# Fused attention and gated MLP on one core: down products, held P.V batches and the first tile of the last output chunk

## The chip, the core and the metric

The kernel runs on one core of a Trainium2 chip. The metric is the time of one execution in microseconds (us) on the device, as the median of several runs. Engines are called as in the profile: PE is TensorE's matmul, PEld its weight load, DVE is VectorE, ACT is ScalarE, POOL is GpSimd, SP is SyncE.

## The reference

The input `x` has 2048 rows of 640 values. It is normalised by row, and the normalised rows feed two branches whose product is added to `x`:

```python
xn = _layernorm(x, axis=-1)
# A: 32 heads of 20 columns
qkv = (xn @ wqkv).reshape(B, S, 3, H, Dh).transpose(2, 0, 3, 1, 4)
scores = einsum("bhqd,bhkd->bhqk", q, k) * Dh ** -0.5
o = einsum("bhqk,bhkd->bhqd", softmax(scores), v)
s = o.transpose(0, 2, 1, 3).reshape(B, S, D) @ wo
# B: F = 1728
h = sigmoid(xn @ w_gate) * (xn @ w_up)
g = silu(h @ w_down)
return x + s * g
```

All inputs and the output are bf16.

## The kernel before

The kernel is written as an instruction order for each engine, and the order comes from a planner in Python that runs when the program is built. The planner keeps a clock for PE (`pe[0]`), models ACT and DVE as queues of tasks with durations (`act`, `dve`), and decides at each step what PE does next.

**Passes.** The queries are cut into four chunks of 512 (`NQC`), the heads into eight groups of four (`NG`, `GH`): 32 passes. A pass holds 64 banks, one bank being the scores of 128 keys against 512 queries of one head, in one PSUM bank. PE computes scores by four row groups at once (L1280). The exponentials of a chunk of three or two banks are one ACT instruction (L1306), alternating between the PSUM sets `sc0` and `sc1`. A further bank can be put into one of two work banks (`misc0`, `misc1`, tile `spare`); DVE then computes its exponential by a cubic polynomial in four steps (L1326, L1347, L1351, L1357). `pv` (L1483) multiplies the probabilities by V, two banks for each head in a batch, and accumulates into `oacc`, the one PSUM bank for it. At the end of a pass DVE copies `oacc` out (`normalise`, L804), and the sums go through DRAM by POOL's DMAs to be inverted and spread.

**Jobs.** All else that PE has to do is a job, a generator that asks for a work bank, for something to be known, or for the time of its next matmul: Q, K and V products, `gateup_job` (gate and up products of one tile of 128 hidden columns into `hT`, with a tanh on ACT and a DVE product at L688), `down_job` (the products of `hT` with `w_down`, accumulated over the 14 tiles of the hidden dimension, L717, then tanh and a DVE product), `out_job` (the output projection of a finished chunk, L751) and the last chunk's jobs. The edge tile of 64 hidden columns is computed for two chunks at once, so an odd chunk's edge tile is made first, with the chunk before it. A job takes a work bank unless `spare_wanted` keeps it for DVE's scores. PE's time for a matmul of `n` columns in the down and output products is `mm_time(n)`.

**Zeros.** Where PE would have little to do, `zero_add` gives it a product with a zero matrix, added to `oacc` while its sum is open (L1459), or into a work bank that nobody uses (`unused`, L1465). `streamed()` is the planner's PE time within the last 3400 ns.

**The end.** The last pass is cut into parts of 256, 128 and 128 queries (`PARTS`). `part_job` computes the output projection of five of the eight head groups ahead for the four output tiles of the last chunk, gates it and has POOL add `x` by DMA (L791), so that `ahead[:, t4, :]` holds that part of the sum. `last_job` then turns the last pass's `oacc` copy (`oev`) with an identity product (L922), inverts the denominators (`rq`, L928), spreads them (`rb`, L933), turns them back (L950), scales (`oT`, L957), multiplies by the remaining rows of `wo` (L912), gates (`gated`, L997, two halves of 320 columns; for the last tile in one piece, L979), and `summed` adds `ahead` on DVE and has SP write the tile (L1001, L1002). The copy of the last part is on ACT (L897), planned by `take_part(len(PARTS) - 1, pe[0])` after the loop.

Of the kernel before, what the change touches and what calls it, by code (L numbers as in the profile page):

```python
# [12 lines left out]
ALU = mybir.AluOpType  # L13
# [3 lines left out]
PARTS = ((0, 256), (256, 128), (384, 128))  # L17
HEAD = 32
GH = 4
# [39 lines left out]
def kernel(  # L59
# [11 lines left out]
    nc = tc.nc  # L71
# [3 lines left out]
    S, D = x2.shape  # L75
# [3 lines left out]
    NFT = (F + P - 1) // P  # L79
# [4 lines left out]
    NQC = S // QC  # L84
    KT = S // P
# [6 lines left out]
    out_view = out2.rearrange("(p t) d -> p t d", t=TT)  # L92
# [84 lines left out]
    with tc.tile_pool(name="setup", bufs=1) as sp, \  # L177
# [167 lines left out]
        for word in ORDER.split():  # L345
            name, _, other = word.partition(":")
            kind, _, t = name.partition(".")
# [16 lines left out]

    MM5, MM3, MM1 = 216.0, 136.0, 70.0
    INTO = {"score": 100.0, "pv": 100.0, "fill": 100.0}
    WINDOW, ENOUGH, ZEROS, RESTED = 3400.0, 2500.0, 16, 400.0
    PE_OUT, SEM = 260.0, 70.0
    EXP_COL, EXP_FIX, EXP_LAG = 1 / 1.2, 52.0, 260.0
    DMA_WAIT, LANDED = 3400.0, 4000.0  # L370
# [48 lines left out]
    pe = [0.0]  # L419
# [27 lines left out]
    def streamed():  # L447
        while streams and streams[0][0] <= pe[0] - WINDOW:
            streams.pop(0)
        return sum(x[1] for x in streams)  # L450
# [7 lines left out]
    banks = [Cell(0.0), Cell(0.0)]  # L458
# [9 lines left out]
    def spare_wanted():  # L468

        free = sum(c.t is not None and c.t <= pe[0] for c in banks)  # L470
        return (free == 1 and not pressed() and next_round[0] - pe[0] < (KEEP_SPARE if at_bank[0] < SPARE_END else KEEP_LATE)
                and dve.backlog + dve.t - next_round[0] < D_BACKLOG)

    EARLY = 2
# [1 line left out]
    def pressed():  # L476
        return at_bank[0] <= EARLY * PER_PASS and any(x.due < at_bank[0] and x.left > 0.0 and (x.asks is None or x.asks[0] != "mm")
                                           for x in flight + jobs[:1])
# [163 lines left out]
    hTs, h_cells, d_cells, hEs = {}, {}, {}, {}  # L642
# [50 lines left out]
            h_cells.setdefault(c + k, []).append(tnh_free[-1])  # L693

    def mm_time(n):
        return max(n / 2.4 + 3.0, 100.0)

    def down_pieces(k):
        return [(t4, max(t4 * D, k * QC), min((t4 + 1) * D, (k + 1) * QC)) for t4 in range(QC // P)
# [2 lines left out]
    def down_job(c, k):  # L702
        last = c == NQC - 1
        yield "known", lambda: (bulk[0] == NFT and pe[0] > bulk_t[0] + LANDED and len(h_cells.get(c, [])) == NFT
                                and (not last or front() >= PER_PASS * (NG * c + k // 2 + 1)))
        yield "wait", h_cells[c]
        hT = hTs[c]
        if last:
            gq = gq_last[:, k * QC:(k + 1) * QC]
        else:  # L710
            gq = glu[0].tile([P, QC], FP32, tag="gqr", bufs=4, name="gq")
        held, psd = yield "bank",
        for t4, f0, f1 in down_pieces(k):
            for kf in range(NFT):
                rows = slice(0, P) if kf < NFT - 1 else slice(EDGE * (c % 2), EDGE * (c % 2 + 1))
                h_in = hT[:, kf, :] if kf < NFT - 1 else hEs[c]
                nc.tensor.matmul(psd[:, f0 - k * QC:f1 - k * QC], lhsT=h_in[rows, t4 * P:(t4 + 1) * P],  # L717
                                 rhs=glu[1][rows, kf, f0 - t4 * D:f1 - t4 * D], start=(kf == 0), stop=(kf == NFT - 1),
                                 skip_group_check=True)
                yield "mm", mm_time(f1 - f0), (f1 - f0) / 2.4  # L720
        d_cells.setdefault(c, []).append(Cell(pe[0]))
        made = {}

        def tanh():
            made["t"] = wk.tile([P, QC], BF16, tag="tnh", bufs=2, name="td")
            nc.scalar.activation(out=made["t"], in_=psd, func=ACT.Tanh, scale=0.25)  # L726

        def finish():
            nc.vector.scalar_tensor_tensor(out=gq, in0=made["t"], scalar=1.0, in1=psd, op0=ALU.add, op1=ALU.mult)
            if not last:  # L730
                nc.gpsimd.dma_start(out=gq_dram[c, :, k * QC:(k + 1) * QC], in_=gq)

        turned = act.add(480.0, [Cell(pe[0] + PE_OUT + 100.0), *tnh_free[-2:-1]], tanh, 0, EXP_LAG)
        tnh_free.append(dve.add(606.0, [turned], finish, 1))
        give_bank(held, tnh_free[-1])
        gq_cells[c, k] = tnh_free[-1]
# [29 lines left out]
    gq_last = kT_all[:, 0:3, :].rearrange("p g s -> p (g s)").bitcast(FP32)[:, 0:4 * D]  # L766
# [121 lines left out]
    def take_part(u, done):  # L888
        q0, width = PARTS[u]
        part = taken_parts[u] = {}  # L890

        def copy():
            part["oev"] = glu[0].tile([P, QC], FP32, tag="gqr", bufs=4, name="oev")[:, 0:width]
            if u < len(PARTS) - 1:
                nc.vector.tensor_copy(out=part["oev"], in_=oacc[:, q0:q0 + width])
            else:
                nc.scalar.activation(out=part["oev"], in_=oacc[:, q0:q0 + width], func=ACT.Identity)  # L897

        if u < len(PARTS) - 1:
            part["cell"] = dve.add(60.0 + width, [Cell(done + PE_OUT)], copy, -1)  # L900
        else:
            part["cell"] = act.add(52.0 + width * EXP_COL, [Cell(done + PE_OUT)], copy, -1, EXP_LAG)
        return part["cell"]

    def last_job(u):
# [13 lines left out]
        else:  # L919
            held, pd = yield "bank",  # L920
# [44 lines left out]
        for k, t4 in enumerate(tiles):  # L965
            got = []
            if final:
                if k:
                    outs = psum.tile([P, 3, 512], FP32, tag="sc0", bufs=1, name="outs")
                    for h in range(2):  # L970
                        out_mm(outs[:, h, 0:HALF], t4, h, NG - 2)
                        yield "mm", MM3
                for h in range(2):
                    out_mm(outs[:, h, 0:HALF], t4, h, NG - 1)
                    yield "mm", MM3

                def gate(t4=t4, outs=outs):
                    gq = gq_last[:, t4 * D:(t4 + 1) * D].rearrange("p (h d) -> p h d", h=2)
                    nc.vector.scalar_tensor_tensor(out=gq, in0=outs[:, 0:2, 0:HALF], scalar=0.25, in1=gq,  # L979
                                                   op0=ALU.mult, op1=ALU.mult)  # L980

                got.append(dve.add(740.0, [Cell(pe[0] + PE_OUT)], gate, -1))
            else:
                for h in range(2):
                    held, ps = yield "bank",
                    for g in range(PRE, NG):
                        out_mm(ps[:, 0:HALF], t4, h, g)
                        yield "mm", MM3
                    got.append(dve.add(400.0, [Cell(pe[0] + PE_OUT)], lambda t4=t4, h=h, ps=ps: gated(t4, h, ps), 1))
                    give_bank(held, got[-1])  # L990
                got.append(ending)
            dve.add(740.0, [out_cells[(NQC - 1) * 4 + t4], *got],
                    lambda t4=t4: summed(t4), -1 if final else 2)

    def gated(t4, h, ps):
        gq = gq_last[:, t4 * D:(t4 + 1) * D][:, h * HALF:(h + 1) * HALF]
        nc.vector.scalar_tensor_tensor(out=gq, in0=ps[:, 0:HALF], scalar=0.25, in1=gq, op0=ALU.mult, op1=ALU.mult)  # L997

    def summed(t4):
        ot = glu[0].tile([P, QC], FP32, tag="gqr", bufs=4, name="ot").bitcast(BF16)[:, 0:D]  # L1000
# [11 lines left out]
    K_COST, B_COST = 5 * MM5, 0.3 * MM5  # L1012
    GU_COST, DOWN_COST = 10 * MM5, NFT * (MM5 + 10.0)
    OUT_COST, PART_COST = NG * (MM5 + 10.0), 2 * (NG - 3) * MM3
    PART_DUE = [LAST-48 + 8 * t4 for t4 in range(4)]
    LAST_DUE = [e - 12 for e in ENDS[1:]] + [NB]
    WO_FROM, BULK_EVERY, bulk_t = 2, 6, [0.0]
    K_DUE, Q_DUE, B_DUE, V_DUE, OUT_DUE = -60, -50, -36, 6, 4 * PER_PASS
# [51 lines left out]
    glu = []  # L1070
# [114 lines left out]
    def held_job():  # L1185
        return any(x.asks is not None and x.asks[0] == "mm" and x.left < x.cost - 1 for x in flight)
# [245 lines left out]
    def pv_batch():  # L1432

        p = pv_pass[0]
        if p >= len(steps) - 1 + len(PARTS):
            return None
        if sum(pv_count[0]) == 0 and not (oacc_free[0].t is not None and oacc_free[0].t <= pe[0]):
            return None
        batch = []
        for j in range(GH):  # L1440
            mine = []
            for x in ready_p[j]:
                b, buf, i = x
                if unit(b) > p or len(mine) == 2:
                    break
                c, v = buf.made, v_cells.get((b % PER_PASS // GH, steps[min(p, len(steps) - 1)][1]))
                if c.t is not None and c.t + SEM <= pe[0] and v is not None and v.t is not None and v.t <= pe[0]:
                    mine.append(x)
            if len(mine) < 2:
                return None  # L1450
            batch.append(mine)
        return batch
# [61 lines left out]
    while pv_pass[0] < len(steps) - 1 + len(PARTS):  # L1514
# [37 lines left out]
        if b0 < NB and not stuck and alone(room):  # L1552
            idle = False
            credit = min(credit + per_bank(b0), 3000.0)
            continue
        batch = pv_batch()
        cost = PV_TIME + (INTO["pv"] if mode[0] != "pv" else 0.0)
        if batch and (cost <= room or held >= HELD):
            pv(batch)
# [23 lines left out]
        times = [until, pe[0] + 150.0] + [t + SEM for t in soon if t is not None]  # L1583
        pe[0] = min(t for t in times if t > pe[0] + 1.0)

    oacc_free[0] = take_part(len(PARTS) - 1, pe[0])
    while flight or jobs or timed or act.queue or dve.queue:
        advance(pe[0])
        if not fill(len(steps) - 1):
# [32 lines left out]
```

## Time and profile before

| | |
|---|---|
| median of 3 runs | 881.26 us (879.89 to 881.51) |
| the profiled execution, its own time | 878.75 us |
| its span in the profile | 877.1 us |
| granted clock of PE | 0.999 |
| ACT / DVE / PE busy | 861.9 / 837.9 / 799.4 us |
| exponentials on ACT | 355 of three banks, 356 of two |
| banks on DVE | 271 |

A busy time is the union of an engine's instructions. In a row of groups, the number after the bar is busy time and the mean of one instruction in ns, then the idle time just before these instructions and what ended it. In a row of the timeline, the first number is the start and the second the length of a stretch of equal instructions, in us.

### The profile page before, as it was taken

What the parts mean: (1) busy time and instruction counts of PE and PEld (TensorE: products, weight loads), DVE (VectorE), ACT (ScalarE), POOL (GpSimd) and SP (SyncE); (2) the same over time, 40 slices, a digit from 0 to 9 for tenths busy, and PEclk for the clock granted to TensorE, in tenths of its full rate; (3) what the DMA queues carried; (4) which work ended last, traced back from release to release, by engine and by line L of the source; (5) the groups of instructions that cost most, each with busy time, mean ns of one, the idle gap of its engine ahead of it and who ended that gap; (6) DMA issues with size and microseconds to landing.
All of it is one profiled execution on the core that took longest, in us unless ns stands there. A gap on an engine that the chain in (4) does not pass through costs nothing.

```text
span 877.1 us, 16778 instructions
## 1 busy us (share of the span) xinstructions
PE 799.4 (91%) x6358; PEld 286.2 (33%) x6440; DVE 837.9 (96%) x1164; ACT 861.9 (98%) x832; POOL 170.0 (19%) x314
## 2 busy tenths in 40 slices
PE   8999899999998999999999999989989989999997
PEld 3434333332222333222223332232223332233344
DVE  7799999999999999999999999999999999999996
ACT  7999999999999999999999999999999999999996
POOL 8401111101111113211101133111112231111110
PEclk9999999999999999999999999999999999999999
DMA  8212231125542124223321235313211443320111
GB/s 320 62 49 66 72 108 36 33 59 142 155 130 68 28 68 108 38 59 74 73 60 39 68 83 86 72 29 84 57 35 50 101 71 80 71 52 21 26 34 47
DMA packets 107303, 63.86 MB, mean 73 GB/s; under 512 B 78674, under 2 KB 101030, under 8 KB 107130
## 3 DMA queue, kind: packets, MB, share of 16 engines
q1 hardware_dynamic: 95270, 46.96, 20.1%
q0 software_dynamic: 11952, 15.83, 8.5%
q8 instruction: 50, 0.82, 0.4%
q14 instruction: 31, 0.25, 0.1%
HBM read 49.94 MB, written 16.11 MB: 75 GB/s over the span
## 4 chain that ended last, share of the span: by engine, by line
ACT 64%; issue 17%; PE 11%; DVE 6%; DMA 1%; POOL 0%; SPq 0%; ACTq 0%; DVEq 0%; POOLq 0%
ACT p L1306 60%; PE sc L1280 3%; ACT tnh L679 3%; PE work L667 2%; PE work L717 2%; PE oacc L1483 2%; DVE du L1351 1%; DVE dy L1326 1%; ACT td L726 1%; DVE p L1357 1%; DVE du L1347 1%; DMA x_sb<-in_A_x_dram 1%; DVE stats L261 1%; POOL x_sb L284 0%; PE oacc L1459 0%
## 5 line engine op out<-in xcount | busy, mean ns | idle before, releaser
L1306 ACT ACTIVATE p<-sc 128x1536 bf16<-128x1536 f32 x711 | 823.1, 1382 | 1.3 <-PE sc L1280 1.2
L1280 PE MATMUL sc<-qT,kT_all 21*128 21x512 bf16 (+2 forms) x1892 | 278.1, 369 | 55.1 <-ACT p L1306 48.0
L1326 DVE TENSOR_SCALAR dy<-spare 128x512 f32<-128x512 f32 x271 | 184.9, 683 | 14.2 <-PE spare L1280 12.0
L1280 PEld LDWEIGHTS <-kT_all 21*128 21x128 bf16 x2176 | 90.4, 91 | 293.8 <-issue 282.5
L1351 DVE SCALAR_TENSOR_TENSOR du<-du,dy 128x1024 f32<-128x1024 f32 (+1 forms) x166 | 169.3, 1021 | 1.3
L1347 DVE SCALAR_TENSOR_TENSOR du<-dy 128x1024 f32<-128x1024 uint16 (+1 forms) x159 | 168.5, 1060 | 1.2
L1357 DVE SCALAR_TENSOR_TENSOR p<-du,dy 128x1024 uint16<-128x1024 f32 (+1 forms) x152 | 167.2, 1100 | 1.4
L1483 PE MATMUL oacc<-p,v_all 128*21 128x512 bf16 (+2 forms) x2176 | 157.2, 370 | 0.6 <-issue 0.3
L1280 PE MATMUL spare<-qT,kT_all 21*128 21x512 bf16 (+2 forms) x284 | 103.7, 373 | 0.5 <-issue 0.3
L808 POOL DMA_DIRECT2D den_dram<-oev x30 | 18.0, 600 | 354.1 <-DVE oev L804 342.7
L717 PE MATMUL work<-wd,hT 128*128 128x512 bf16 (+3 forms) x410 | 75.2, 301 | 1.9 <-DVE dy L1326 1.2
L667 PE MATMUL work<-xnT,wg 128*128 128x512 bf16 (+1 forms) x262 | 74.0, 383 | 1.9 <-issue 0.6
L667 PE MATMUL work<-xnT,wu 128*128 128x512 bf16 (+1 forms) x266 | 69.8, 381 | 2.1 <-DVE dy L1326 0.6
L824 POOL DMA_DIRECT2D rl<-rec_dram x120 | 60.9, 544 | 52.2 <-DMA rec_dram<-den 47.4
L1483 PEld LDWEIGHTS <-v_all 128*21 128x21 bf16 x2176 | 31.8, 90 | 59.3 <-issue 57.3
L1459 PE MATMUL oacc<-xnT,zero 128*128 128x512 bf16 x124 | 42.7, 385 | 3.0 <-issue 2.4
L717 PEld LDWEIGHTS <-hT 128*128 128x128 bf16 x416 | 30.7, 97 | 39.0 <-issue 29.7
L818 POOL DMA_DIRECT2D rec_dram<-den x30 | 16.4, 547 | 132.9 <-DVE den L817 125.1
L679 ACT ACTIVATE tnh<-work 128x512 bf16<-128x512 f32 x54 | 39.3, 728 | 0.0
L138 PE MATMUL work<-xnT,wqd 128*120 128x512 bf16 (+1 forms) x115 | 35.0, 393 | 0.6 <-DVE hT L688 0.3
L688 DVE SCALAR_TENSOR_TENSOR hT<-tnh,work 128x512 bf16<-128x512 bf16 x52 | 35.3, 679 | 0.1
L667 PEld LDWEIGHTS <-wu 128*128 128x128 bf16 (+1 forms) x280 | 23.4, 98 | 36.7 <-issue 18.8
(132 smaller groups left out, 573.7 us busy)
## 6 DMA issues: line engine op xcount, KB each, us to landing
wg<-in_B_w_gate_dram SPq DMA_DIRECT2D x52, 160.0 KB
wu<-in_B_w_up_dram SPq DMA_DIRECT2D x52, 160.0 KB
rl<-rec_dram POOLq DMA_DIRECT2D x120, 64.0 KB, 2.5
qT<-q_dram SPq DMA_DIRECT2D x31, 128.0 KB
gq_dram<-gq POOLq DMA_DIRECT2D x15, 256.0 KB, 2.3
gqr<-gq_dram SPq DMA_DIRECT2D x15, 256.0 KB
kT_all<-k_dram SPq DMA_DIRECT2D x28, 128.0 KB
wd<-in_B_w_down_dram SPq DMA_DIRECT2D x13, 160.0 KB
```

Source lines behind the costliest of these rows:

```text
L667: nc.tensor.matmul(ps[EDGE * k:EDGE * (k + 1), :] if both else ps, lhsT=w[:, kd, 0:EDGE if both else P], rhs=xnT[:, kd, (c + k) * QC:(c + ...
L679: nc.scalar.activation(out=made["t"][0:fsz, :], in_=psg[0:fsz, :], func=ACT.Tanh, scale=0.5)
L717: nc.tensor.matmul(psd[:, f0 - k * QC:f1 - k * QC], lhsT=h_in[rows, t4 * P:(t4 + 1) * P], rhs=glu[1][rows, kf, f0 - t4 * D:f1 - t4 * D], s ...
L824: nc.gpsimd.dma_start(out=t["rl"][32 * j:32 * j + 32, :], in_=rec_dram[n, j:j + 1, :].to_broadcast([32, QC]))
L1280: nc.tensor.matmul(ps[:, c0:c0 + n], lhsT=kT_all[rows, g, kt * P:(kt + 1) * P], rhs=qTs[qc, g][rows, q0:q0 + n], start=True, stop=True, ti ...
L1306: nc.scalar.activation(out=buf.tile(), in_=ps, func=ACT.Exp, bias=EXP_BIAS, scale=exp_scale)
L1326: nc.vector.tensor_scalar(out=pair.y[:, i * 512:(i + 1) * 512], in0=ps, scalar1=LEAST, scalar2=None, op0=ALU.max)
L1347: nc.vector.scalar_tensor_tensor(out=t["u"][:, a:e], in0=t["f"][:, a:e], scalar=CUBE_2, in1=t["f"][:, a:e], op0=ALU.add, op1=ALU.mult)
L1351: nc.vector.scalar_tensor_tensor(out=t["u"][:, a:e], in0=t["u"][:, a:e], scalar=CUBE_1, in1=t["f"][:, a:e], op0=ALU.add, op1=ALU.mult)
L1357: nc.vector.scalar_tensor_tensor(out=t["p"][:, a:e], in0=t["u"][:, a:e], scalar=CUBE_SCALE, in1=t["y"][:, a:e], op0=ALU.mult, op1=ALU.add)
L1459: nc.tensor.matmul(oacc, lhsT=zero, rhs=xnT[:, 0, 0:QC], start=not begun, stop=not begun, skip_group_check=True)
L1483: nc.tensor.matmul(oacc[32 * j:32 * j + 1 + Dh, q0:q0 + width], lhsT=v_all[:, kt, GH * g + j, 0:1 + Dh], rhs=buf.ap[:, i, c0:c0 + width], ...
```

## The change

The change has five parts.

1. `down_job` waits at its start for all hidden tiles but the last made, and then, ahead of each product, for that product's tile. The products run in the order in which the tiles are made, so an odd chunk takes the edge tile first. `mm_time` loses its floor of 100 ns: 128 columns count 56 ns and no longer 100.
2. `spare_wanted` keeps the last free work bank for DVE's scores only while `streamed()` exceeds `STARVED`, 1500 ns.
3. In the main loop the last P.V batch of a pass is held while neither work bank is free, no job is in the middle of its products, and fewer than 19 banks of probabilities are waiting. While it is held, zeros can be added to `oacc`, whose sum is still open.
4. The first tile of the last chunk (`t4 == 0`) is no longer summed on DVE and written by SP. After its second gating POOL adds the gated tile into `ahead[:, 0, :]` by a DMA from SBUF to SBUF, and a second DMA of POOL writes `ahead[:, 0, :]` to the output, with the cast to bf16.
5. The last part's copy is planned as if `oacc` were done 200 ns sooner.

```diff
-    WINDOW, ENOUGH, ZEROS, RESTED = 3400.0, 2500.0, 16, 400.0
+    WINDOW, ENOUGH, ZEROS, RESTED, STARVED = 3400.0, 2500.0, 16, 400.0, 1500.0
...
-        return (free == 1 and not pressed() and next_round[0] - pe[0] < (KEEP_SPARE if at_bank[0] < SPARE_END else KEEP_LATE)
+        return (free == 1 and not pressed() and streamed() > STARVED and next_round[0] - pe[0] < (KEEP_SPARE if at_bank[0] < SPARE_END else KEEP_LATE)
                 and dve.backlog + dve.t - next_round[0] < D_BACKLOG)
...
     def mm_time(n):
-        return max(n / 2.4 + 3.0, 100.0)
+        return n / 2.4 + 2.7
...
-        yield "wait", h_cells[c]
+        made_in = [(NFT - 1 if c % 2 and not i else i - c % 2, x) for i, x in enumerate(h_cells[c])]
+        yield "wait", [x for _, x in made_in[:-1]]
...
         for t4, f0, f1 in down_pieces(k):
-            for kf in range(NFT):
+            for i, (kf, h_cell) in enumerate(made_in):
+                yield "wait", [h_cell]
                 rows = slice(0, P) if kf < NFT - 1 else slice(EDGE * (c % 2), EDGE * (c % 2 + 1))
                 h_in = hT[:, kf, :] if kf < NFT - 1 else hEs[c]
                 nc.tensor.matmul(psd[:, f0 - k * QC:f1 - k * QC], lhsT=h_in[rows, t4 * P:(t4 + 1) * P],
-                                 rhs=glu[1][rows, kf, f0 - t4 * D:f1 - t4 * D], start=(kf == 0), stop=(kf == NFT - 1),
+                                 rhs=glu[1][rows, kf, f0 - t4 * D:f1 - t4 * D], start=(i == 0), stop=(i == NFT - 1),
                                  skip_group_check=True)
...
                 got.append(ending)
+            if t4 == 0:
+                continue
             dve.add(740.0, [out_cells[(NQC - 1) * 4 + t4], *got],
                     lambda t4=t4: summed(t4), -1 if final else 2)
 
     def gated(t4, h, ps):
         gq = gq_last[:, t4 * D:(t4 + 1) * D][:, h * HALF:(h + 1) * HALF]
         nc.vector.scalar_tensor_tensor(out=gq, in0=ps[:, 0:HALF], scalar=0.25, in1=gq, op0=ALU.mult, op1=ALU.mult)
+        if h == 1 and t4 == 0:
+            nc.gpsimd.dma_start(out=ahead[:, t4, :], in_=gq_last[:, t4 * D:(t4 + 1) * D], accum_op=ALU.add)
+            nc.gpsimd.dma_start(out=out_view[:, (NQC - 1) * 4 + t4, :], in_=ahead[:, t4, :])
...
         batch = pv_batch()
+        if (batch and b0 < LAST and held < 19 and sum(pv_count[0]) == GH * KT - 2 * GH and not held_job()
+                and all(c.t is None or c.t > pe[0] + 0.0 for c in banks)):
+            batch = None
...
-    oacc_free[0] = take_part(len(PARTS) - 1, pe[0])
+    oacc_free[0] = take_part(len(PARTS) - 1, pe[0] - 200.0)
```

## The prediction

> **What bounds the kernel now.** I read the page's engine totals first, then ScalarE (ACT) by stage, its groups by shape and its waits, and last the timeline of the final 20 us, because four of the five edits act there.
>
> Engine totals, then busy time by stage (PE, PEld, DVE, ACT, POOL, each with its instruction count; then granted clock, DMA share, GB/s):
>
> ```profile
> PE 799.4 (91%) x6358; PEld 286.2 (33%) x6440; DVE 837.9 (96%) x1164; ACT 861.9 (98%) x832; POOL 170.0 (19%) x314
> ...
> 220.00:420.00 200.00, 183.72 (x1386) 60.69 (x1403) 195.45 (x257) 200.00 (x191) 38.11 (x67) 1.00 0.34 81
> ...
> 868.70:877.10 8.40, 3.11 (x47) 1.73 (x47) 4.53 (x9) 0.29 (x2) 0.00 (x0) 0.94 0.17 59
> ```
>
> ACT is busy for the whole of every 200 us stage from 220 us on, and after its last exponential it is nearly idle: the kernel is a saturated ACT from 27.7 to 868.7 us, then a tail of 8.4 us in which VectorE (DVE) and TensorE (PE) hand work to each other. ACT's shapes and waits:
>
> ```profile
> L1306 ACT ACTIVATE p<-sc 128x1536 bf16<-128x1536 f32 x355 | 566.4, 1596 | 1.2 <-PE sc L1280 1.2
> L1306 ACT ACTIVATE p<-sc 128x1024 bf16<-128x1024 f32 x356 | 416.3, 1170 | 0.1
> ```
>
> Three banks against two differ by 1596 - 1170 = 426 ns, so a bank of 512 columns taken from ACT is worth 0.43 us. ACT waits for scores only 1.2 us. Records overlap, though: in the trace the next exponential starts 1.330 us after one of three banks begins and 0.903 us after one of two. 355 x 1.330 + 356 x 0.903 + 74 tanh x 0.48 = 829 us, against a stretch of 841 us, so 12 us are lost in pieces, nearly all under 0.3 us. Only one is large:
>
> ```profile
> 856.01 0.68 DVE L1326 TENSOR_SCALAR dy<-spare 128x512 f32<-128x512 f32 x1
> 856.14 1.25 PE L1465 MATMUL unused<-xnT,zero 128*128 128x512 bf16 x3
> 856.61 0.41 DVE L895 COPY oev<-oacc 128x256 f32<-128x256 f32 x1
> 857.46 0.49 PE L922 MATMUL work<-identf,oev 128*128 128x128 f32 x2
> 858.10 0.42 PE L1280 MATMUL sc<-qT,kT_all 21*128 21x128 bf16 x12
> 858.65 1.45 ACT L1306 ACTIVATE p<-sc 128x1536 bf16<-128x1536 f32 x1 [0.64 <-PE sc L1280]
> ```
>
> Three zeros go to a work bank that DVE is still reading, the turn of `oev` (L922) stands behind them, the scores behind that, and ACT starts 0.64 us late (0.86 us against its rhythm). Then the tail on DVE:
>
> ```profile
> 869.81 0.49 DVE L997 SCALAR_TENSOR_TENSOR kT_all<-work,kT_all 128x320 f32<-128x320 f32 x1 [0.58 <-PE work L912]
> 870.22 0.17 DVE L928 RECIPROCAL rq<-side 128x4 f32<-128x4 f32 x1
> 870.43 0.23 DVE L933 COPY rb<-rq 128x128 f32<-128x128 f32 x1
> 870.57 0.82 DVE L1001 TENSOR_TENSOR ot<-kT_all 128x640 bf16<-128x640 f32 x1
> 871.30 0.29 DVE L957 TENSOR_TENSOR oT<-oev,side 128x128 bf16<-128x128 f32 x1
> 871.51 0.82 DVE L1001 TENSOR_TENSOR ot<-kT_all 128x640 bf16<-128x640 f32 x1
> 872.25 0.82 DVE L979 SCALAR_TENSOR_TENSOR kT_all<-outs,kT_all 128x640 f32<-128x640 f32 x1
> 873.10 0.83 DVE L1001 TENSOR_TENSOR ot<-kT_all 128x640 bf16<-128x640 f32 x1
> ```
>
> From 870.4 us DVE works without a gap: whatever its order puts there moves the end. Its last sum ends at 873.93; the write is issued at 873.95, lands at 875.7, and ending the program takes 1.3 us more.
>
> **The change, part by part.** The instruction order of the changed kernel is the planner's; it is the same as before up to ACT's 237th instruction (246 us), so nothing earlier can differ.
>
> *Planner edits (spare bank given up when PE starved, shorter time for 128-column products, down products ahead of the last tile, held batches).* Counted over the whole program: one bank of exponentials goes from ACT to DVE (356 exponentials of two banks become 355 and one of a single bank, and that one is the last). ACT: -0.43 us. DVE: one more first step (0.68 us) and three arithmetic steps over 512 more columns (about 0.53 each): 2.3 us, beside ACT's work, since DVE has 39 us free; if that cover failed, one DVE operation would delay a buffer by at most 0.7 us. Zeros into `oacc` go from 163 to 185, `unused` ones from 6 to 0: 16 more at 0.216 us start to start, 3.5 us of PE, which has 16 us free in each 200 us stage. A held batch stands in front of nothing but the next passes' batches; who waits for it is DVE's copy of `oacc` and, through the probability buffers, ACT. A down product that begins early puts a wait for one DVE tile (0.68 us) in PE's queue, with the next scores behind it. Neither wait is in the trace; its nearest row is ACT's 1.2 us for scores in all 711 exponentials. I take no net change, and +1.5 to -1.5 us (an eighth of the 12 us lost) as bounds, since the order is drawn anew for 600 us.
>
> *The stall at 856.9.* In the new order no `unused` zeros stand there; both turns of `oev` come after the 12 scores. That returns 0.64 to 0.86 us. But the last `part_job` half (5 products, 0.68 us of PE) now stands in front of these scores and its bank must be free, so between 0 and -0.86 I take -0.64.
>
> *The first output tile by DMA.* One DVE sum (0.81 us at 866.46) goes; DVE waited 0.52 us for PE right behind it, so this frees nothing on the path. Two POOL DMAs come: 320 KB added into `ahead`, then written out. The nearest rows land 3.8 us (320 KB with add, L791) and 2.3 us (256 KB plain) after issue. The second gating of tile 0 should end near 867.3 (its products stand behind the scores of the last exponential but one). 867.4 + 3.8 + 0.1 + 2.3 to 3.8 = 873.6 to 875.1, before the last write's 875.7: hidden.
>
> *The tail.* With the last exponential 0.43 us shorter the last P.V starts near 868.2 instead of 868.63. The second half of tile 2 (3 products, 0.41 us) now precedes the turn L950, but the turn was held by `rb`, so it starts at 870.5 (870.71 before) and the final `oT` at 871.07 (871.30). But then DVE's order has that half's gating (0.45 start to start) between `oT` and the second sum: 871.07 + 0.21 + 0.45 = 871.73, + 0.74 = 872.47 for the last gate against 872.25. So the tail ends 0.2 us later, the 0.43 us already spent in it. Bounds: -0.4 (the gating fits into a wait) and +0.95 (PE's three products delay the turn in full). The copy listed 0.2 us sooner leaves one zero behind the turn instead of two around it: inside this sum.
>
> Sum on the profiled execution: 878.75 (span 877.1 and 1.65 around it) - 0.64 + 0.2 = 878.3. The median of the runs, 881.26, lies 2.5 above the profiled one; the same -0.44 there gives **880.8**.
>
> [...]
>
> **Rivals.** About 0.2% (1.76 us) is what a measurement of this kernel can tell from no change.
>
> *Faster: the small losses shrink.* 12 us are lost where scores come late. The planner's 100 ns for a 128-column product is really 56 ns in the trace, and with starved PE work gets a second bank. If a fifth of the loss goes (2.4 us) on top of the 0.44: 878.4. For: the corrected time. Against: one bank, not several, moved to DVE. 15%.
>
> *Faster: the clock.* The program's first zeros start 0.427 us apart from 1.1 to 5.7 us, and 0.216 apart afterwards: a slow stretch of 4.6 us. PE is 92% busy, so a like stretch amid the passes would cost ACT about half of that, 2.1 us; one in each plain run would explain most of their 2.5 us above the profile, and 16 more zeros would end it: 880.8 - 2.1 = 878.7. Against: clock 1.00 wherever it can be seen. 10%. [...]
>
> *Slower: zeros and held batches in front of scores.* If each of the 22 added `oacc` zeros holds the next scores for its 0.216 us, +4.8 us less 0.44: 885.6; with the loss per zero that the trace allows (12 us over 169 zeros, 0.07 us), +1.5: 882.3. It decides once ACT's wait for scores exceeds some 3 us; before, 169 zeros left it at 1.2. 9%.
>
> *Slower: the DMA pair ends the kernel.* If the add from SBUF to SBUF takes twice the 3.8 us and the write 3.8, it lands at 867.4 + 7.6 + 0.1 + 3.8 = 878.9, 3 us behind the last write: 883.9. It decides above 8.3 us for the pair. Against: both rows are far below. 5%.
>
> *The change does nothing* is out: the order differs.
>
> **How the numbers follow.** Forecast 61%, alone spanning 879.2 to 882.5 (the +-1.5 and the tail's and stall's bounds). The two faster rivals hold 25%, the slower two 14%. The first faster one lands past the 0.2% bound; of the second and of the forecast's lower edge a part does: faster 0.26. Slower by over 0.2%: the DMA pair, half of the zeros, a little of the forecast's edge: 0.12. Within: 0.62. The range reaches to the faster rivals and to the mild form of the zeros: 878.2 to 882.6.
>
> **What would show it.** Right: ACT's wait for scores at or below 1.2 us with no 0.64 us row near 857; the last exponential about 0.4 us sooner relative to its predecessors; an L997 row between the final `oT` and the second sum, the last gate 4.2 to 4.5 us after the last P.V's start (3.6 before); the POOL write landed before SP's last. Wrong: an ACT wait of 3 us and more; a last release by POOL's DMA; granted clock below 1.00 before the tail; or the stretch of ACT shorter than 839 us.

## The result, and the profile after

The changed kernel takes 878.13 us (median of 21 runs, 877.78 to 881.0), the kernel before, run beside it, 880.68 us (21 runs, 878.79 to 885.91). The ratio is 0.9973, 95% interval 0.9963 to 0.9983: 2.4 us faster. The profiled executions differ by less: 877.90 us after 878.75, spans of 876.2 and 877.1 us.

The single runs show why the median moved further than the profile. Of the 21 runs of before, seven lie between 878.79 and 879.03, the others at 879.89 and above; of the changed kernel's 21 runs, 20 lie between 877.78 and 878.46, and one took 881.0 us at a granted clock of 0.994. So before has two kinds of execution, and its profile shows the shorter kind. PE's granted clock, listed below for each run, parts the two kinds: in the kernel before the shorter kind has 0.998 to 1.000, the longer kind 0.993 to 0.998. They meet at 0.998 because the figure is a mean over the whole span, with the end, where PE has nothing left to do (the last stage below shows 0.88, with 0.50 from 874.08 us on).

The share of the longer kind varies, 14 of 21 runs here and 13 of 29 beside e9 to e12, and with it the median of before (880.68 and 879.22 us). The shorter runs agree, 878.9 us in both. So 0.8 us of the gain lies between runs at full clock; the rest depends on how often the clock of before falls.

Engine totals and stages of the changed kernel, as shown of before (PE, PEld, DVE, ACT, POOL, then granted clock, DMA share, GB/s):

```profile
PE 815.2 (93%) x6456; PEld 287.3 (33%) x6456; DVE 837.0 (96%) x1169; ACT 861.6 (98%) x832; POOL 171.9 (20%) x316
...
220.00:420.00 200.00, 186.53 (x1413) 61.72 (x1412) 196.14 (x250) 200.00 (x190) 38.20 (x67) 1.00 0.32 78
...
867.40:876.20 8.80, 3.46 (x51) 2.02 (x49) 5.34 (x11) 0.54 (x2) 1.41 (x2) 0.88 0.48 112
```

ACT is as saturated as before. PE is 16 us busier, but the earlier trace lacks records (6440 weight loads, 6358 matmuls). In e1, whose trace of the same kernel lacks none, PE is busy for 813.0 us, so most of the 16 us is missing records. ACT's shapes:

```profile
L1313 ACT ACTIVATE p<-sc 128x1536 bf16<-128x1536 f32 x355 | 564.1, 1589 | 0.6 <-PE sc L1287 0.6
L1313 ACT ACTIVATE p<-sc 128x1024 bf16<-128x1024 f32 x355 | 412.9, 1163 | 0.1
```

One two-bank exponential less (the last has one bank), and the wait for scores is 0.6 instead of 1.2 us. Around 857 us, where ACT had started 0.64 us late:

```profile
855.56 4.83 ACT L1313 ACTIVATE p<-sc 128x1536 bf16<-128x1536 f32 x4
856.35 0.42 DVE L897 COPY oev<-oacc 128x256 f32<-128x256 f32 x1
856.56 0.85 PE L785 MATMUL work<-wo_pad,oT 128*128 128x320 bf16 x5
857.35 0.42 PE L1287 MATMUL sc<-qT,kT_all 21*128 21x128 bf16 x12
857.70 0.71 PE L924 MATMUL work<-identf,oev 128*128 128x128 f32 x4
```

Four exponentials follow each other without a gap, and the turn of `oev` stands behind the 12 scores. The tail on DVE:

```profile
868.71 0.49 DVE L1001 SCALAR_TENSOR_TENSOR kT_all<-work,kT_all 128x320 f32<-128x320 f32 x1 [0.58 <-PE work L914]
...
869.47 0.82 DVE L1008 TENSOR_TENSOR ot<-kT_all 128x640 bf16<-128x640 f32 x1
870.31 0.29 DVE L959 TENSOR_TENSOR oT<-oev,side 128x128 bf16<-128x128 f32 x1
870.51 0.48 DVE L1001 SCALAR_TENSOR_TENSOR kT_all<-work,kT_all 128x320 f32<-128x320 f32 x1
871.03 0.82 DVE L1008 TENSOR_TENSOR ot<-kT_all 128x640 bf16<-128x640 f32 x1
871.77 0.82 DVE L981 SCALAR_TENSOR_TENSOR kT_all<-outs,kT_all 128x640 f32<-128x640 f32 x1
872.62 0.83 DVE L1008 TENSOR_TENSOR ot<-kT_all 128x640 bf16<-128x640 f32 x1
```

The gating of tile 2 (L1001 at 870.51) stands between the final `oT` and the second sum.

A budget of the two profiles follows. ACT's work is the sum of its instructions at their rhythm (1.330 us for three banks, 0.903 for two, 0.477 for one bank or a tanh); what is lost is the stretch from ACT's first exponential to the end of its last (its start plus its rhythm), less that work; the tail is the rest of the span.

| us | before | after | difference |
|---|---|---|---|
| first exponential starts | 27.66 | 27.50 | -0.16 |
| ACT's work | 828.92 | 828.49 | -0.43 |
| lost in the stretch | 11.93 | 11.37 | -0.56 |
| tail | 8.55 | 8.81 | +0.26 |
| span | 877.06 | 876.17 | -0.89 |

So the profiles explain 0.9 us, about what parts the shorter runs of before (near 878.9) from those of the changed kernel (878.1). The other 1.6 us or so is the longer kind of execution.

### The profile page after: what moved, and what is told of

Same layout as the page of the kernel before. It is cut to its first block, busy times and chain, and to the rows that moved or that the text cites. A ratio compares the mean times of both kernels' runs of the same rounds, so it can differ in the third digit from the quotient of the medians.

```text
span 876.2 us, 16902 instructions
## 1 busy us (share of the span) xinstructions
PE 815.2 (93%) x6456; PEld 287.3 (33%) x6456; DVE 837.0 (96%) x1169; ACT 861.6 (98%) x832; POOL 171.9 (20%) x316
## 4 chain that ended last, share of the span: by engine, by line
ACT 60%; issue 17%; PE 10%; DVE 10%; DMA 1%; POOL 0%; SPq 0%; ACTq 0%; DVEq 0%; POOLq 0%
ACT p L1313 56%; PE sc L1287 3%; ACT tnh L679 3%; DVE dy L1333 2%; DVE du L1358 2%; PE oacc L1490 2%; PE work L667 2%; DVE p L1364 2%; DVE du L1354 2%; ACT td L728 1%; PE work L719 1%; DMA x_sb<-in_A_x_dram 1%; DVE stats L261 1%; PE oacc L1466 1%; DVE hT L688 1%
## 5 line engine op out<-in xcount | busy, mean ns | idle before, releaser
L719 PE MATMUL work<-wd,hT 128*128 128x512 bf16 (+3 forms) x416 | 77.1, 302 | 0.4 <-DVE dy L1333 0.4
L667 PE MATMUL work<-xnT,wg 128*128 128x512 bf16 (+1 forms) x280 | 77.3, 383 | 0.1
L1466 PE MATMUL oacc<-xnT,zero 128*128 128x512 bf16 x185 | 61.9, 386 | 0.6 <-DVE oev L806 0.6
```

Source lines behind the costliest of these rows:

```text
L667: nc.tensor.matmul(ps[EDGE * k:EDGE * (k + 1), :] if both else ps, lhsT=w[:, kd, 0:EDGE if both else P], rhs=xnT[:, kd, (c + k) * QC:(c + ...
L1466: nc.tensor.matmul(oacc, lhsT=zero, rhs=xnT[:, 0, 0:QC], start=not begun, stop=not begun, skip_group_check=True)
```

## Experiments: where the clock falls

**e1: the kernel before once more.** No edit.

> The kernel before, unchanged, for its runs one by one. Theory C (clock): from 291.75 to 294.17 us PE has little to do in it, and in part of the executions PE's clock falls there; those take 1.5 to 3 us more and show a mean granted clock of 0.993 to 0.997, the others lie near 878.9 at 0.998 to 1.000. Theory S (schedule): the gain of the change is spread over the order of all 600 us; the runs of before spread by 2 us for reasons outside the kernel, and their clocks are all 0.998 to 1.000.

Measured: 12 runs, median 879.97 us, ratio 1.0004 (0.9989 to 1.0018). Four took 878.6 to 878.9 at clocks of 0.998 to 1.000, one 879.4 at 0.998, and seven 879.9 to 883.0 at 0.993 to 0.997. In the 35 runs of the kernel before that stood beside e1 to e4, 15 lie at 878.4 to 879.4, all at 0.998 or more, and 20 at 880.0 to 883.1, in steps: about 880.4, 881.6, 883.0. The profile of e1 is one of the longer kind. Its stages (columns as above):

```profile
496.70:500.14 3.44, 3.42 (x34) 1.35 (x30) 3.17 (x5) 3.44 (x4) 0.10 (x1) 1.00 0.42 133
500.14:503.55 3.41, 2.53 (x27) 0.97 (x25) 3.41 (x6) 3.41 (x5) 0.39 (x1) 1.00 0.40 139
503.55:506.96 3.41, 3.41 (x12) 0.97 (x10) 3.38 (x4) 2.34 (x4) 1.28 (x3) 0.50 0.23 79
506.96:510.40 3.44, 3.44 (x32) 0.83 (x30) 2.11 (x3) 3.31 (x4) 0.00 (x0) 1.00 0.24 79
```

After a stretch in which PE was busy for 2.53 of 3.41 us its clock is 0.50 for 3.41 us; PE then runs without a pause and still serves ACT too slowly, and ACT is idle for 1.07 us in that time. So the clock falls, but not at 292 us, as theory C had put it: it fell at the end of the eighteenth pass. There, too, PE waits for a copy of `oacc` while both work banks are held:

```profile
501.23 0.61 PE L1483 MATMUL oacc<-p,v_all 128*21 128x512 bf16 x8
501.77 0.23 PE L717 MATMUL work<-wd,hE 64*128 64x128 bf16 x1
501.93 0.39 PE L1280 MATMUL sc<-qT,kT_all 21*128 21x512 bf16 x2
501.94 0.39 PE L1280 MATMUL spare<-qT,kT_all 21*128 21x512 bf16 x1
502.92 0.38 PE L1459 MATMUL oacc<-xnT,zero 128*128 128x512 bf16 x1 [0.60 <-DVE oev L804]
```

The half clock lasted 3.41 us here, 6.83 in e9, 13.65 in e4. PE had not been idle ahead of it: it had been busy for 74% of the 3.41 us.

PE's busy time alone does not decide it. In the profile of before the clock stayed full behind these two stretches, the second at the same end of a pass:

```profile
292.37:295.78 3.41, 1.95 (x13) 0.70 (x14) 3.41 (x6) 3.41 (x4) 0.58 (x1) 1.00 0.01 2
500.59:504.00 3.41, 2.52 (x25) 0.95 (x24) 3.41 (x6) 3.41 (x5) 0.54 (x1) 1.00 0.38 138
```

The 1.95 us can't be put down to missing records: e1 has 1.99 us in the like stretch (291.92 to 295.33), and stays at full clock behind it.

**e2: two zeros at the end of the tenth pass.** One `if` in `pv`, ahead of the last batch; the planner does not see it, so nothing else moves:

```diff
         most = full(p)
+        if p == 9 and sum(pv_count[0]) == GH * KT - 2 * GH:
+            for _ in range(2):
+                nc.tensor.matmul(oacc, lhsT=zero, rhs=xnT[:, 0, 0:QC], start=False, stop=False, skip_group_check=True)
```

> The kernel before with two products with zeros more, put ahead of the last P.V batch of the tenth pass alone (at about 291.75 us); nothing else in the order differs. Theory C: the slower kind of execution is gone or rare; the median falls by 1.5 to 2 us to about 879 and nearly all runs lie within 0.6 us. Theory S: no change (ratio 1.000), or up to 0.2 us slower, since the zeros stand in front of scores; the spread stays.

Measured: 12 runs, median 878.97 us, ratio 0.9995 (0.9984 to 1.0007). Nine lie at 878.6 to 879.1 at 0.998 or more, three at 880.3 to 882.8 at 0.993 to 0.996. The profile fell on one of these, with a clock of 0.50 from 504.03 to 507.45 us: the end of the eighteenth pass again. By the ratio this is no change; by the share of longer runs (3 of 12, against 7 of 12 in e1) it looked like half a cure, which 12 runs can't settle.

**e9: the same at the end of the eighteenth pass alone** (`p == 17`).

> The kernel before with two products with zeros more at the end of the eighteenth pass alone (501.2 us); the place at the end of the tenth pass (291.75 us) is left as before. Theory C2, two places: what e2 repaired, this leaves open, so 4 to 6 of 12 executions are at a lower clock and take 880 to 881.5, the others lie near 878.8. Rival, one place: only the eighteenth pass matters, and at most 1 of 12 is slower, as in e5.

Measured: 12 runs, median 880.29 us, ratio 1.0003 (0.9992 to 1.0014). Five at 878.8 to 879.0, three at 880.2 to 880.4, four at 881.5 to 881.9. The profile has the fall at the other place:

```profile
290.77:294.18 3.41, 2.21 (x22) 0.65 (x19) 3.38 (x5) 3.41 (x5) 0.00 (x0) 1.00 0.00 0
294.18:297.59 3.41, 2.97 (x10) 0.79 (x10) 3.41 (x6) 2.43 (x3) 1.14 (x2) 0.50 0.01 2
297.59:301.00 3.41, 3.41 (x17) 0.66 (x15) 0.82 (x1) 2.47 (x2) 0.00 (x0) 0.50 0.02 2
```

PE was busy for 2.21 of 3.41 us at the end of the tenth pass, and the half clock lasted 6.83 us; ACT lost 14.83 us in its stretch where the profile of before lost 11.93. So there are two places, and each alone still makes longer runs.

Why only a part of the executions lose their clock is not shown. In the profiles of before, of the changed kernel and of e9 the clock changes only at whole multiples of 3.413 us after its first record (in before at 255 of them, from 5.65 to 876.05 us; in the changed kernel at 254, from 7.10 to 874.08; in e9 at 85 and 87, from 4.04 to 294.18 and 301.00), and the same place of the program lies differently under this grid in each execution: the last batch of the tenth pass starts 0.6 us ahead of a stretch in the profile of before, and 1.2 us into one here. That the place under the grid decides fits the two kinds, but no run tests it.

**e5: both** (`p in (9, 17)`).

> The kernel before with two products with zeros more ahead of the last P.V batch of the tenth pass and two ahead of that of the eighteenth (501.2 us, where the profile of e1 shows PE at half clock from 503.55 to 506.96 us); nothing else differs. Theory C2 (the clock falls at ends of passes where PE has least to do): at least 9 of 12 executions lie within 0.4 us of 878.8 at a clock of 0.998 or more, median near 878.8, 1.4 us below before. Theory S (order): the spread of before stays, median about 880, as the zeros change no order.

Measured: 12 runs, median 878.94 us, ratio 0.9988 (0.9979 to 0.9997); all 12 between 878.4 and 879.4, at 0.998 to 1.000. At the second place the stretch after the last P.V batch now reads

```profile
500.40:503.80 3.40, 2.97 (x28) 1.16 (x29) 3.20 (x5) 3.40 (x4) 0.00 (x0) 1.00 0.50 168
503.80:507.20 3.40, 3.23 (x19) 1.01 (x18) 3.40 (x6) 3.40 (x5) 1.68 (x3) 1.00 0.04 11
```

PE is busy for 2.97 us where it had been 2.53, and the clock stays full. Four products, 0.9 us of PE, end the longer kind of execution and take 1.15 us off the median (880.09 beside it). Theory S is out as the whole cause: no order was changed.

**e6: the changed kernel without the zeros of held batches.** The planner's order and clock are kept; only the issue is left out where one batch of the pass is missing, 39 products in all:

```diff
-            nc.tensor.matmul(oacc, lhsT=zero, rhs=xnT[:, 0, 0:QC], start=not begun, stop=not begun, skip_group_check=True)
+            if sum(pv_count[0]) != GH * KT - 2 * GH:
+                nc.tensor.matmul(oacc, lhsT=zero, rhs=xnT[:, 0, 0:QC], start=not begun, stop=not begun, skip_group_check=True)
```

> The changed kernel in its own order, but the 39 products with zeros that the planner put into a sum with one P.V batch left are not issued (22 more than before are added by the change in all). Theory C2: executions at a lower clock come back, in half or more of the runs, median 879 to 881; those at full clock stay near 878.1. Theory S: the order and not the zeros brought the gain: median 877.8 to 878.2, if anything 0.1 to 0.3 us less, since PE has 8 us less to do.

Measured: 6 runs, 885.35 to 893.79, median 889.13 us, ratio 1.0105 (1.0078 to 1.0133), clocks 0.976 to 0.987: worse than any theory had it. In its profile the clock is at half in four places, 23.9 us together, each behind a stretch at the end of a pass in which PE was busy for 1.95 to 2.38 of 3.4 us:

```profile
319.80:323.19 3.39, 1.95 (x20) 0.73 (x19) 3.39 (x6) 3.39 (x4) 0.54 (x1) 1.00 0.20 77
323.19:333.43 10.24, 10.24 (x56) 3.31 (x53) 7.05 (x8) 6.90 (x6) 1.26 (x3) 0.50 0.02 4
531.40:534.81 3.41, 2.00 (x24) 0.52 (x25) 3.41 (x6) 3.41 (x4) 0.00 (x0) 1.00 0.59 189
534.81:538.23 3.42, 3.42 (x24) 1.26 (x16) 3.42 (x5) 2.72 (x3) 1.47 (x2) 0.50 0.47 54
```

The stretch of ACT loses 21.03 us, 9.66 more than with the zeros: 0.40 us for each us of half clock, which also fits the steps of the runs of before (3.41 x 0.4 = 1.4 us). The order of the changed kernel is the same here, so it needs these zeros to keep its clock.

They are not all the change's. By the order of the products in the traces, the kernel before has 20 zeros of this kind (counted in e1), the changed kernel 39. The four places are the ends of the third, eleventh, nineteenth and twenty-fifth pass; at the third the kernel before has the same four zeros, at the others it has one, none and none, the changed kernel five, three and three. At the ends of the tenth and eighteenth pass, where before loses its clock, the changed kernel has no zero of this kind, and the profile of e6 keeps its clock there. There it is the order that differs. At the end of the tenth pass before has only scores behind the last batch:

```profile
291.75 0.61 PE L1483 MATMUL oacc<-p,v_all 128*21 128x512 bf16 x8
292.83 0.39 PE L1280 MATMUL sc<-qT,kT_all 21*128 21x512 bf16 x2 [0.47 <-ACT p L1306]
294.17 0.39 PE L1280 MATMUL sc<-qT,kT_all 21*128 21x512 bf16 x3 [0.95 <-ACT p L1306]
```

and the changed kernel has gate products of a job there:

```profile
290.18 0.61 PE L1490 MATMUL oacc<-p,v_all 128*21 128x512 bf16 x8
290.72 0.62 PE L667 MATMUL work<-xnT,wg 128*64 128x512 bf16 x4
291.60 0.84 PE L667 MATMUL work<-xnT,wg 128*64 128x512 bf16 x6
```

So, as far as these profiles show, the changed kernel keeps its clock by both: at the two places of before by the new order, at other ends of passes by the zeros. No run takes the two apart.

**e3 and e4: the holding left out of the changed kernel, and put alone into the kernel before.** The edit is the three lines `if (batch and ...): batch = None`, removed and added.

> The changed kernel without the holding of P.V batches; its order at the end of the tenth pass is that of before again (last P.V batch, then only scores until the down products). Theory C: the spread of before comes back, runs near 878.5 and runs 1.5 to 3 us above at a lower clock, median about 880, ratio to before 0.998 to 1.000. Theory S: the median stays within 0.5 us of the changed kernel's 878.1, ratio 0.997.

> The kernel before with the holding of P.V batches alone. Theory C: the slower kind of execution is gone, median 878.3 to 879.2, ratio to before 0.997 to 0.9985, spread under 0.8 us. Theory S: between 0 and a fifth of the gain (ratio 0.9995 to 1.000), and the spread stays.

Measured: e3 has 12 runs of 880.85 to 884.97, median 882.58 us, ratio 1.0028 (1.0016 to 1.0040); three at 0.999 took 880.9 to 881.0, the rest 882.2 and more at 0.994 to 0.998. The longer kind is back, as theory C said; but even its shorter runs are 2.8 us above the changed kernel, which no theory had. e4: seven of 12 runs at 880.0 to 880.4 and a clock of 0.999 or 1.000, five at 881.0 to 885.7 at 0.992 to 0.996, median 880.34 us, ratio 1.0022 (1.0003 to 1.0040). Both theories are wrong on it: the holding alone makes the kernel no faster. It draws an order with two banks fewer on DVE (269 against 271), that is 0.9 us more work for ACT, and with a place of its own where the clock falls (716.3 us, for 13.65 us). So the gain is that of the order which the planner edits give together; e3 and e4 each draw another order and give no price of the holding alone. Why the shorter runs of e3 are 2.8 us up was not taken apart.

## Experiments: the other parts

The 878.13 us of the changed kernel, with which e7, e8 and e12 are compared, are from other runs than theirs. The shorter runs of before, with a median of 878.9 us beside it and of 878.8 and 878.9 beside these experiments, tie the two together to about 0.2 us.

**STARVED** does nothing here: without it the program of the changed kernel is the same, instruction for instruction.

**e7: down products that wait for all hidden tiles.**

```diff
-        yield "wait", [x for _, x in made_in[:-1]]
+        yield "wait", [x for _, x in made_in]
```

> The changed kernel with down products that wait for all hidden tiles again, as before. Its order differs from the changed kernel's only from ACT's 768th instruction on (the last chunk); one bank goes back from DVE to ACT. By the step of the prediction that prices the bank at 0.43 us: 0.3 to 0.9 us slower than the changed kernel, 878.4 to 879.0. Rival: the bank is worth nothing because the last stretch is redrawn anyhow: 877.9 to 878.3.

Measured: 11 runs, median 879.46 us (878.70 to 880.04), 1.3 us above the changed kernel's; ratio to before 0.9996 (0.9987 to 1.0005). Nine ran at 0.998 or more, so this is not the clock. The profile's budget has ACT's work back at 828.92 (+0.43) and the tail at 8.56 (-0.25); its loss can't be compared, since the clock fell in it at 107.5 us, a place where this order is still the changed kernel's. Starting ahead of the last tile changes the order only from 793.7 us on, moves the bank, and is worth more than the 0.43 of that bank; where the rest comes from is open.

**e11: the floor of 100 ns for a product of 128 columns put back.**

```diff
-        return n / 2.4 + 2.7
+        return max(n / 2.4 + 3.0, 100.0)
```

> The changed kernel with the planner's floor of 100 ns for a product of 128 columns put back; its order differs from PE's 4343rd instruction on, and it has 20 zeros less in oacc. Theory M (the corrected time makes scores come in time): executions at full clock are 0.5 to 1.5 us above 878.1. Rival (a redraw without direction): within 0.5 us of 878.1 at full clock; some may lose clock, since zeros are fewer.

Measured: 6 runs, 882.94 to 889.90, median 885.78 us, ratio 1.0072 (1.0052 to 1.0093), clocks 0.990 to 0.998. Both theories are far too small. In the profile, that of the longest run, DVE's queue stands for 3.36 us at a reciprocal (L819) that waits for a DMA, PE waits 3.17 us for DVE behind it, the clock is at half from 358.3 to 371.95 us, and the tail is 11.9 us long, since its order leaves more of the last tiles' products and gatings behind the last exponential. A wrong duration for one product draws a worse order; that is a draw, not a price of the 44 ns.

**e8: the first tile summed on DVE again, the last copy listed as before.** The two DMAs and the `continue` go, and `pe[0] - 200.0` is `pe[0]` again. Up to PE's last 14 products, at 868.5 us, nothing changes.

> The changed kernel with the first output tile of the last chunk summed on DVE and written by SP again and with the last copy listed as before. The order puts that sum last of all on DVE, behind the last tile's. Theory T (the tail is DVE's queue): the end comes 0.7 to 0.9 us later, 878.8 to 879.0. Rival, by the prediction: the sum lies beside a wait for PE and the edit frees nothing, within 0.2 us of 878.1.

Measured: 11 runs, median 878.99 us (878.68 to 879.44), ratio to before 0.9988 (0.9980 to 0.9997): 0.86 us above the changed kernel, as theory T had it. DVE in the end:

```profile
871.57 0.82 DVE L981 SCALAR_TENSOR_TENSOR kT_all<-outs,kT_all 128x640 f32<-128x640 f32 x1
872.30 1.55 DVE L1003 TENSOR_TENSOR ot<-kT_all 128x640 bf16<-128x640 f32 x2
```

Two sums follow the last gate instead of one. From the end of ACT's last exponential, the last sum starts 0.61 us later than in the changed kernel, but the span ends 1.02 later. The other 0.41 is in the program's end: SP checks one semaphore after the other, 0.06 us each, and with four writes on SP the last write's is the third in that list, so that seven checks follow its landing (875.74 to 876.16 us in the profile of before); with three it is the last one (875.28 in that of the changed kernel).

**e10: the same edits in the order of before**, on top of e5.

> The kernel of e5 (before with two products with zeros at each of the two places) with the first output tile of the last chunk summed by DMA and the last copy listed sooner. The prediction's step, that in the order of before this frees nothing: within 0.2 us of e5's 878.9, tail after ACT's last exponential as in e5. Rival: a DVE sum less is 0.7 to 0.8 us less, as e8 showed for the changed kernel's order: 878.1 to 878.3.

Measured: 11 runs, median 878.46 us (878.17 to 878.80), ratio 0.9990 (0.9981 to 0.9998), 0.5 us below e5 (878.94). (The runs of before at full clock took the same beside both, 878.9 and 878.8; the ratios are to all its runs, and hide this.) Between the two expectations, and neither's reason holds: the last sum starts as long after ACT's last exponential as in e5 (4.59 and 4.58 us). What is shorter, by 0.41 us (tail 8.14 against 8.55), is what follows the last write's landing: the list of checks. SP's waits at the end, before and after the change (us in total, times, longest):

```profile
SPq L1617 <- DMA out_dram<-ot: 1.3, 1, 1.3
```

```profile
SPq L1627 <- DMA out_dram<-ot: 0.9, 1, 0.9
```

SP reaches the write's semaphore sooner in the first and waits longer there, with the other checks still ahead of it. The write itself lands equally fast: issue to wake-up is 1.79 us before and 1.80 after.

**e12: the third tile's sum on POOL.** It stands on DVE between the final `oT` and the last gating, so this should have beaten both kernels. The planner's 740 ns for it on DVE become 0, and:

```diff
-        nc.vector.tensor_tensor(out=ot, in0=gq_last[:, t4 * D:(t4 + 1) * D], in1=ahead[:, t4, :], op=ALU.add)
+        (nc.gpsimd if t4 == 2 else nc.vector).tensor_tensor(out=ot, in0=gq_last[:, t4 * D:(t4 + 1) * D], in1=ahead[:, t4, :], op=ALU.add)
```

> The changed kernel with the sum of the last chunk's third output tile on POOL, where it is on DVE between the final oT and the last gating; DVE then has 0.74 us less there. Theory T (the tail is DVE's queue): PE's last products are done 0.5 us before the gating starts, so the end comes 0.3 to 0.6 us sooner, 877.5 to 877.8. Rival: POOL starts late, behind the write of the first tile, takes 1.5 us or more and its tile is written last: 878.0 to 878.6.

Measured: 11 runs, median 879.02 us (878.80 to 879.34), 0.9 us above the changed kernel; ratio to before 0.9992 (0.9982 to 1.0002). The last gate did start sooner, at 871.32 instead of 871.77, but then:

```profile
871.82 1.55 POOL L1008 TENSOR_TENSOR ot<-kT_all 128x640 bf16<-128x640 f32 x1
872.17 1.89 DVE L1008 TENSOR_TENSOR ot<-kT_all 128x640 bf16<-128x640 f32 x1
```

DVE's last sum took 1.89 us instead of 0.83. POOL's sum ended at 873.37, and 0.69 us of DVE's lie behind that, so little of it can have been done before. SP's three writes were issued at 873.40, 873.80 and 874.27, where the last had been issued at 873.48.

## Why the prediction was right or wrong

The forecast was 880.8 us, 0.44 below before and most likely within 0.2%. The changed kernel came out 2.4 us faster, past that bound. The range, 878.2 to 882.6 us, reached that low only to take in the two faster rivals: 878.13 us lies just below its lower edge, and the ratio 0.9973, applied to the 881.26 us from which the prediction started, gives 878.9, inside it. That is luck as far as the forecast's own sum goes: most of the distance came from the clock, to which it gave nothing. By its own steps:

- *The bank, 0.43 us:* right, ACT's work fell by 0.43.
- *The stall at 856.9, -0.64, with no net change from the rest of the order:* right in the profile's sum, -0.56 lost in the stretch, and the waits for scores fell from 1.2 to 0.6. For the median it does not hold, since the new order also keeps the clock where the old one lost it.
- *The tail:* the DVE side came as worked out. The last gate starts 4.24 us after the last P.V batch (4.27 forecast, 3.62 before), and the last sum 0.66 us later after ACT's last exponential. The end of the program was missed: 0.41 us come back because SP's list of checks now ends with the last write. So the tail is +0.26 instead of +0.63 from ACT's end. This and a first exponential that starts 0.16 us sooner make most of the difference between the profiles' 0.89 us and the forecast's 0.44.
- *The first tile by DMA frees nothing:* right on DVE in the order of before, from which it was argued (e10: no change in the last sum's start), wrong in the changed order, where the sum would have been last on DVE (e8: 0.61 us), and wrong on the end of the program (0.41 us in the list of checks, in both). The two DMAs went as priced (issue at 867.40; 3.88 us to the next issue at 871.28; landed before SP's last write).
- *The step that failed* is the transfer to the median: "the same -0.44 there". It took the 2.5 us between the profile of before and its median as an offset that the changed kernel would have too. They are runs with stretches at half clock: e5 ends them without any change of order, and the changed kernel's median is 0.2 us above its profile. The rival "Faster: the clock" had this, with a price of 2.1 us and 878.7 us in all, and even noted that one such stretch in each run would explain most of the 2.5 us. It got 10% because the profile showed a clock of 1.00. The spread of three runs (879.89 to 881.51, all above the profiled 878.75) pointed to it. The rival put the cure down to 16 more zeros; e6 shows that zeros keep the clock at some ends of passes, but at the two places of before it is the new order.
- *"Clock 1.00 wherever it can be seen":* not in the last stage, which shows 0.94, and the first 5.65 us have no record of the clock, though the zeros there start 0.427 us apart.
- *What the added zeros buy:* the forecast gave them no gain, and they keep the clock. Without the 39 zeros of held batches the changed kernel takes 11 us more (e6); 20 zeros of this kind stand in the kernel before too.
- *The rival "zeros and held batches in front of scores"* did not come: ACT's wait for scores went down, not up.
- *The forecast's span, 879.2 to 882.5:* its bounds, simply added, give 878.5 to 883.7.

The signs by which the prediction wanted to be judged came out for it: the wait for scores, the gating between the final `oT` and the second sum, the last gate at 4.24 us, the POOL write landed in time, no fall of the clock ahead of the tail. They are all read from one profile, and what the forecast missed shows only in the spread of the runs.

## What to carry to other kernels

When a kernel's runs lie well above its profiled execution, look for the stretch where PE has least to do, here the ends of passes, before calling the difference an offset: a few filler products there can be worth more than all work saved on the bound engine (here four took 1.15 us off the median in e5, where the bank saved ACT 0.43). Where a planner draws the order, undoing an edit draws another order; an edit that the planner does not see (e2, e5, e6, e9) is the one that tells cause from draw. And count what follows the last write: the order of the final checks was worth as much as a bank (0.41 us against 0.43).

## What the runs showed of the hardware

- PE's clock went to half behind stretches of 3.41 us in which PE was busy for 0.90 us (e11), 1.95 to 2.69 us (e1 to e4, e6, e9) and 2.80 us (e7). Busy time does not decide it: it stayed full behind 1.95 (before), 1.99 (e1) and 2.46 us (e5, from 292.51). It stayed at half for 3.41 (e1, e2, e6), 6.83 (e3, e6, e9), 10.24 (e6) or 13.65 us (e4, e11), all multiples of the first, though PE was often busy without a pause meanwhile (10.24 of 10.24 us in e6).
- What in PE's work keeps the clock is open. An estimate from the PE rows of the traces comes nearer than busy time: count each product as 0.216 us for 512 columns (the time from one zero's start to the next in before), times the rows and columns that its row names, as a share of the 128*128 of a zero. The profiles have 3448 stretches at full clock between the first 20 and the last 10 us; by this estimate the 11 stretches ahead of a fall are among the lowest 43, by busy time among the lowest 305. It is not the whole rule, since the others of the 43 left the clock full (five of the traces lack about 1% of the products). By it a zero (128*128) counts six times a P.V product (128*21).
- Half clock costs this kernel, bound by ACT, 0.38 (e1), 0.40 (e6) or 0.42 us (e9) for each us.
- A sum of two operands in SBUF on DVE took 1.89 instead of 0.83 us beside one of the same kind on POOL that had started 0.35 us before it. Why was not shown.
- A DMA of 320 KB from SBUF to SBUF with an add landed 3.6 us after its issue, about as the same add from DRAM (3.7 us in the same profile).
